# One-token decode on one Trainium2 core: K loaded after half of wq in runs of 16 KB, with a new pattern for its transposes, and wo's first 18 rows as one load

## The chip, the core and the metric

The kernel runs on one core of one Trainium2 chip. The metric is the device time of one execution in microseconds (us); several executions give a median. The profile beside it comes from one profiled execution. Of the engines, TensorE (PE) does the matrix products, VectorE (DVE) the transposes and most elementwise work, ScalarE (ACT) the exponentials and three small loads, GpSimd (POOL) fills constants at the start, and SyncE (SP) issues nearly all loads. All loads are moved by the core's 16 DMA engines.

## The reference

One token passes an attention block and an MLP block side by side. Cut to what matters:

```
xn  = layernorm(x)                                   # x: 1 x 1024
q   = xn @ wq                                        # wq: 1024 x 4096, 32 heads of 128
k,v = last 4096 positions of the caches, 4 kv heads, each shared by 8 heads
p   = softmax(q k^T / sqrt(128));  A = (p v) @ wo    # wo: 4096 x 1024
y   = layernorm(xn);  h = gelu(y @ w1 + b1)          # w1: 1024 x 3584
out = x + A + (h @ w2 + b2)                          # w2: 3584 x 1024
```

Everything is bf16. Each weight and each used cache element is used once, so some 39.9 MB have to come from memory: wq 8 MiB, w1 7, K 4, V 4, w2 7, wo 8.

## The kernel before

**Buffers.** `WA` holds wq, then w2, then wo's last rows. `W1` holds w1, then wo's other rows. `KV` holds K, then V. `KT` holds the transposed K. A load into a used buffer must wait until its readers are done, and that makes the order of the whole kernel.

**Loads.** Nearly all are issued by SP, in program order, and SP stops at each wait. First, without a wait: four K loads (L212, one for each kv head, 1 MiB, each of the 128 partitions getting one run of 8 KB), two halves of wq (L152, 4 MiB each, runs of 32 KB), two halves of w1 (L152, 3.5 MiB each). Then SP waits for the last K transpose (`C["kt"]`) and issues four V loads (L266). It waits for q to be done (`done["q"]`) and issues w2 in two loads. It waits for the first MLP product (`done["h"]`) and issues wo: 10 rows, 8 rows, then eight small loads of one split row (L275, `LOW`), then 6, 4, 2 and 1 rows. ("A row" of wo is here 128 partitions by 1024 columns.) Each load has its own semaphore, and PE waits for it where it first needs the data. Meanwhile ACT issues three small loads of its own at the start: the row x (2 KB), the row b2 (2 KB) and b1 (7 KB) (L161, L165). x and b2 go to the two rows of one tile, `XBRP`, and share the semaphore `s_x`; PE's first matmul waits for both.

**VectorE.** Its program order is: both layer norms and the spreading of xn into `XZ` and `YZ` (L223 to L253), a small constant (L256), then the four K transposes (L261), one for each K load:

```
for i in range(HKV):
    dve.wait_ge(s_k[i], 16)
    C["kt"] = DVE.mark(dve.transpose(KT[:, i * 4096:(i + 1) * 4096], KV[:, i * 4096:(i + 1) * 4096]))
```

A transpose here turns 32 x 32 blocks. After them come the copy of q out of PSUM (L282), its transpose (L284), eight copies into `QBD` (L291), the maximum of the scores, the transpose of the probabilities, and the MLP's GELU.

**TensorE.** Its program order is: x broadcast to all partitions (L373), two opening matmuls (L383), 64 matmuls over wq (L379 with `XZ`; 32 for each half), 28 over w1's first half (L379 with `YZ`), the 32 score matmuls over `KT` (L412, after `d_QBD`), 28 over w1's second half, the probabilities times V (L454), w2 (L464), then wo row by row as its loads land (L424 for 24 rows and for `LOW`, L430 for the last seven). Between the 24th and the 25th row ScalarE moves a part of the sum (L357). VectorE and ScalarE copy the result out (L363), SP stores it (L365).

Of the kernel before, what the change touches and what calls it, by code (L numbers as in the profile page):

```python
# [9 lines left out]
D = 1024  # L10
F = 3584
HQ = 32
HKV = 4
DH = 128
REP = HQ // HKV
SK = 65536
W = 4096
FC = F // 128
KC = D // 128
NQ = HQ * DH  # L20
W1_CHUNKS = [4, 4]
WQ_CHUNKS = [4, 4]
W2_CHUNKS = [16, 12]
WO_CHUNKS = [10, 8, 6, 4, 2, 1]
WO_HEAD = 4
WO_LOW = 18
XW = 136
QG = 520
# [22 lines left out]
def bass_parallel_sum__sliding_block_cached__mixer_channel_mlp__decode_kernel(  # L51
# [17 lines left out]
    pe, dve, act, pool, sp = nc.tensor, nc.vector, nc.scalar, nc.gpsimd, nc.sync  # L69

    def sems(name, n):
        return [nc.alloc_semaphore(f"{name}{i}") for i in range(n)]
# [2 lines left out]
    s_low = nc.alloc_semaphore("s_low")  # L75
    s_w1 = sems("s_w1", len(W1_CHUNKS))
    s_wq = sems("s_wq", len(WQ_CHUNKS))
    s_k = sems("s_k", HKV)
    s_wo = sems("s_wo", len(WO_CHUNKS))
    s_w2 = sems("s_w2", len(W2_CHUNKS))  # L80

    DVE = Track(nc, "S_DVE")
# [5 lines left out]
    def sb(name, shape, d):  # L88
        return nc.alloc_sbuf_tensor(name, shape, d)
# [40 lines left out]
    KV = sb("KV", [128, 16384], bf16)  # L130
    KT = sb("KT", [128, 16384], bf16)
    W1 = sb("W1", [128, KC * F], bf16)
    LOW = KT[0:64, 0:2 * D]
    WA = sb("WA", [128, KC * NQ], bf16)
# [8 lines left out]
    wq_p = A_wq.rearrange("(p r) n -> p r n", r=KC)  # L143
    w2_p = B_w2.rearrange("(p c) n -> p c n", c=FC)
    wo_p = A_wo.rearrange("(p j) n -> p j n", j=32)
    out_rows = out.rearrange("b s (a n) -> (b s a) n", a=2)

    C = {}

    def load_chunks(dst, src, chunks, width, semaphores, c0=0):  # L150
        for j, n in enumerate(chunks):
            sp.dma_start(  # L152
                dst[:, c0 * width:(c0 + n) * width].rearrange("p (c n) -> p c n", c=n),
                src[:, c0:c0 + n, :],
            ).then_inc(semaphores[j], 16)
            c0 += n
# [51 lines left out]
    POOL.mark(pool.memset(PT[:, 1024:1024 + 96], 0.0))  # L208
    C["consts"] = POOL.cnt

    for g in range(HKV):
        sp.dma_start(  # L212
            KV[:, g * 4096:(g + 1) * 4096],
            A_k_cache[0, g, SK - W:SK, :].rearrange("(p i) d -> p (i d)", p=128)).then_inc(s_k[g], 16)
    load_chunks(WA, wq_p, WQ_CHUNKS, NQ, s_wq)
    load_chunks(W1, w1_p, W1_CHUNKS, F, s_w1)

    def dve_wait():
# [37 lines left out]
    DVE.mark(dve.tensor_reduce(  # L256
        out=B32[:, :], in_=identf[:, :].rearrange("p (q r) -> p r q", q=4), axis=AX.X, op=ALU.add))

    for i in range(HKV):
        dve.wait_ge(s_k[i], 16)  # L260
        C["kt"] = DVE.mark(dve.transpose(KT[:, i * 4096:(i + 1) * 4096], KV[:, i * 4096:(i + 1) * 4096]))  # L261

    V = KV[:, :]
    sp.wait_ge(DVE.sem, C["kt"])
# [4 lines left out]
    sp.wait_ge(done["q"], 1)  # L269
    load_chunks(W2, w2_p, W2_CHUNKS, D, s_w2)  # L270
    sp.wait_ge(done["h"], 1)
    load_chunks(W1, wo_p, WO_CHUNKS[:2], D, s_wo)
    low_source = A_wo.rearrange("(u p j) n -> p u j n", u=2, j=32)[:, :, WO_MAIN, :]
    for first in (0, 1, 2, 3, 32, 33, 34, 35):
        sp.dma_start(  # L275
            LOW[first:first + 29:4, :].rearrange("p (u n) -> p u n", u=2),
            low_source[first:first + 29:4]).then_inc(s_low, 16)
    load_chunks(W1, wo_p, WO_CHUNKS[2:WO_HEAD], D, s_wo[2:], WO_LOW)
    load_chunks(WA, wo_p, WO_CHUNKS[WO_HEAD:], D, s_wo[WO_HEAD:], FC)

    dve.wait_ge(done["q"], 1)
# [127 lines left out]
    for b in range(2):  # L409
        for n in range(16):  # L410
            g, j = n // 4, n % 4
# [66 lines left out]
    c0 = 0  # L478
    for j, n in enumerate(WO_CHUNKS):
        if c0 == WO_LOW:  # L480
# [43 lines left out]
```

## Time and profile before

| | |
|---|---|
| median of 3 runs (lowest to highest) | 100.55 us (100.5 to 102.49) |
| the profiled execution: its own time, its span | 100.35 us, 99.1 us |
| busy: PE, DVE, ACT, POOL | 70.5, 37.5, 5.7, 6.5 us |
| DMA | 39.89 MB, mean 402 GB/s over the span |
| mean granted TensorE clock | 0.992 of full speed |

The span runs from the first to the last instruction; the time also holds 1.25 us around it. Busy times are sums over the span and say nothing of what waits for what; the DMA slices, the chain of waits and the start and landing times of single loads do. "Landing" is the time from the issue of a load until its semaphore is complete.

### The profile page before, as it was taken

Reading aid. Unit: us, or ns where it says so; the run is one execution under the profiler, and the core shown is the slowest. Engines: PE = TensorE matmul, PEld = TensorE weight load, DVE = VectorE, ACT = ScalarE, POOL = GpSimd, SP = SyncE. Lnnn points to the kernel's source line nnn. Section 1 sums busy time; section 2 is a strip of 40 time slices with the busy share of each in tenths; the row PEclk is TensorE's granted clock in tenths of the full one; section 3 lists DMA queues with packets and bytes.
Section 4 is the critical chain, followed back from the end, with each engine's and each line's share of the span. In section 5 each row is a group of like instructions: output and inputs, shape, how many; then the busy total and the mean of one; then the engine's idle time right before and its main releaser. Section 6 shows DMA issues by size and latency. Waiting matters only on the chain.

```text
span 99.1 us, 1197 instructions
## 1 busy us (share of the span) xinstructions
PE 70.5 (71%) x341; PEld 28.4 (29%) x341; DVE 37.5 (38%) x56; ACT 5.7 (6%) x11; POOL 6.5 (7%) x26
## 2 busy tenths in 40 slices
PE   0021000305999999999999999799999999979532
PEld 0000000002334433334444344233335445422210
DVE  0007998999999900091002543440024010000001
ACT  0500004200000000000000040000000000000021
POOL 6990000000000000000000000000000000000000
PEclk9999999999999999999999999999999999999996
DMA  2999999999999889889799999998999999999960
GB/s 26 397 426 418 430 436 436 489 476 463 450 423 397 370 382 544 370 382 544 301 423 420 423 522 423 423 423 370 476 476 422 388 397 427 423 402 440 397 256 4
DMA packets 3286, 39.89 MB, mean 402 GB/s; under 512 B 594, under 2 KB 596, under 8 KB 980
## 3 DMA queue, kind: packets, MB, share of 16 engines
q1 hardware_dynamic: 3076, 39.85, 95.0%
q10 hardware_dynamic: 208, 0.01, 0.1%
q8 instruction: 1, 0.02, 0.1%
q14 instruction: 1, 0.01, 0.0%
HBM read 39.86 MB, written 0.00 MB: 402 GB/s over the span
## 4 chain that ended last, share of the span: by engine, by line
DMA 46%; PE 40%; SPq 10%; issue 2%; DVE 0%
PE PS L379 31%; DMA WA<-in_A_wo_dram 26%; DMA WA<-in_A_wq_dram 20%; PE PS L412 7%; SPq L275 6%; SPq L152 2%; SPq L212 2%; PE PS L383 1%; PE PS L436 1%; DVE Pb L363 0%; PE PS L430 0%
## 5 line engine op out<-in xcount | busy, mean ns | idle before, releaser
L379 PE MATMUL PS<-WA,XZ 128*128 x64 | 17.9, 433 | 5.6 <-DMA WA<-in_A_wq_dram 5.2
L261 DVE STREAM_TRANSPOSE KT<-KV 128x4096 bf16<-128x4096 bf16 x4 | 17.4, 4409 | 0.0
L379 PE MATMUL PS<-W,YZ 128*128 x56 | 13.0, 381 | 0.0
L464 PE MATMUL PS<-WA,GT 128*64 x56 | 12.5, 380 | 0.0
L379 PEld LDWEIGHTS PS<-WA,XZ 128*128 x64 | 6.9, 108 | 17.0 <-issue 13.2
L383 PE MATMUL PS<-XBRP,HOT 1*128 1x512 bf16 x6 | 2.5, 454 | 9.5 <-DVE XZ L253 9.5
L454 PE MATMUL PS<-KV,PT 128*128 x32 | 8.5, 378 | 0.7 <-issue 0.7
L464 PEld LDWEIGHTS PS<-WA,GT 128*64 x56 | 6.0, 110 | 5.8 <-issue 1.2
L379 PEld LDWEIGHTS PS<-W,YZ 128*128 x56 | 5.2, 96 | 7.5 <-issue 2.5
L412 PE MATMUL PS<-KT,QBD 128*128 128x512 bf16 x32 | 7.1, 379 | 0.0
L424 PE MATMUL PS<-W,OT 128*32 128x512 bf16 x48 | 5.7, 380 | 1.8 <-DMA W<-in_A_wo_dram 1.8
L363 DVE CAST Pb<-PS 64x256 bf16<-64x256 f32 x1 | 0.4, 417 | 16.1 <-PE PS L430 16.1
L373 PE MATMUL PS<-XBRP,onesb 1*128 1x512 bf16 x2 | 1.0, 605 | 6.7 <-DMA XBRP<-in_B_b_dram 6.7
L297 DVE TENSOR_REDUCE MX<-PS 128x1 f32<-128x512 f32 x2 | 1.4, 692 | 10.0 <-PE PS L412 10.0
L454 PEld LDWEIGHTS PS<-KV,PT 128*128 x32 | 3.1, 96 | 6.1 <-issue 2.7
L223 DVE BATCH_NORM_STATS2 BN<-PS 128x6 f32<-128x512 f32 x2 | 1.3, 688 | 7.7 <-PE PS L373 7.7
L412 PEld LDWEIGHTS PS<-KT,QBD 128*128 128x128 bf16 x32 | 3.1, 98 | 3.7 <-issue 0.2
L383 PEld LDWEIGHTS PS<-XBRP,HOT 1*128 1x128 bf16 x6 | 0.5, 94 | 11.5 <-issue 11.5
L342 DVE SCALAR_TENSOR_TENSOR QBD<-PS,REC,GMASK 32x512 f32<-32x512 f32 x1 | 0.7, 739 | 7.9 <-PE PS L383 7.9
L424 PEld LDWEIGHTS PS<-W,OT 128*32 128x32 bf16 x48 | 2.1, 97 | 5.3 <-DMA W<-in_A_wo_dram 2.8
L282 DVE CAST Pb<-PS 128x512 bf16<-128x512 f32 x1 | 0.7, 692 | 7.4 <-PE PS L383 7.4
L308 ACT ACTIVATE Pb<-PS,NMB 128x1024 bf16<-128x1024 f32 x1 | 1.1, 1114 | 40.1 <-DVE NMB L305 40.1
(79 smaller groups left out, 33.4 us busy)
## 6 DMA issues: line engine op xcount, KB each, us to landing
WA<-in_A_wq_dram SPq DMA_DIRECT2D x2, 4096.0 KB, 24.4
W<-in_B_w_dram SPq DMA_DIRECT2D x2, 3584.0 KB, 41.0
KV<-in_A_k_cache_dram SPq DMA_DIRECT2D x4, 1024.0 KB, 7.9
KV<-in_A_v_cache_dram SPq DMA_DIRECT2D x4, 1024.0 KB, 20.6
WA<-in_B_w_dram SPq DMA_DIRECT2D x1, 4096.0 KB, 27.2
WA<-in_B_w_dram SPq DMA_DIRECT2D x1, 3072.0 KB, 34.2
W<-in_A_wo_dram SPq DMA_DIRECT2D x1, 2560.0 KB, 21.4
W<-in_A_wo_dram SPq DMA_DIRECT2D x1, 2048.0 KB, 25.9
```

The lines of the kernel that those rows point to most:

```text
L152: sp.dma_start(dst[:, c0 * width:(c0 + n) * width].rearrange("p (c n) -> p c n", c=n), src[:, c0:c0 + n, :],).then_inc(semaphores[j], 16)
L212: sp.dma_start(KV[:, g * 4096:(g + 1) * 4096], A_k_cache[0, g, SK - W:SK, :].rearrange("(p i) d -> p (i d)", p=128)).then_inc(s_k[g], 16)
L223: DVE.mark(dve.bn_stats(out=BN[:, 12 * n + 6 * i:12 * n + 6 * i + 6], in_=src[:, 512 * i:512 * i + 512]))
L261: C["kt"] = DVE.mark(dve.transpose(KT[:, i * 4096:(i + 1) * 4096], KV[:, i * 4096:(i + 1) * 4096]))
L275: sp.dma_start(LOW[first:first + 29:4, :].rearrange("p (u n) -> p u n", u=2), low_source[first:first + 29:4]).then_inc(s_low, 16)
L297: DVE.mark(dve.tensor_reduce(out=MX2[:, b:b + 1], in_=S[:, 512 * b:512 * b + 512], axis=AX.X, op=ALU.max))
L379: pe.matmul(bank(n), lhsT=vec[:, bass.ds(t + width * k, 128)], rhs=rhs_at(k, t), start=False, stop=False, skip_group_check=True)
L383: return pe.matmul(bank(n), lhsT=HOT[:, 8:136], rhs=XB[0:1, 0:8, :], start=start, stop=not start, skip_group_check=True)
L412: last = pe.matmul(bank(3 + b), lhsT=QBD[:, g * 512 + j * 128:g * 512 + j * 128 + 128], rhs=K5[:, g, 16 * b:16 * b + 16, j, :], start=(n = ...
L424: ins = pe.matmul(acc(a), lhsT=window(vec, c, a), rhs=rhs[:, a * 512:(a + 1) * 512], start=False, stop=stop, tile_position=(0, 32 * a), sk ...
L454: pe.matmul(bank(1), lhsT=PT[:, bass.ds(i * 256 + u * 32, 128)], rhs=V4[:, :, bass.ds(i * 8 + u, 1), :], start=False, stop=False, skip_gro ...
L464: pe.matmul(bank(7, 64), lhsT=GT[:, bass.ds(i * (4 * STEP) + (LEAD + STEP * (c0 + u) - ROW - a), 64)], rhs=W2[:, bass.ds(i * 4 * D + ((c0 ...
```

## The change

- **Order of loads.** SP issues wq's first half first, then K, then wq's second half and w1.
- **K in two loads.** Each load brings two kv heads, 2 MiB, with one run of 16 KB for each partition: partition 2m+g gets 64 consecutive positions of head g of the pair. There are two K semaphores in place of four.
- **The transposes.** There are still four of 128 x 4096 bf16, two behind each load, and they read contiguous columns. Because the partitions hold other positions, the output goes through a rearranged view of `KT`, so that `KT` ends up with the old layout. Within a block of 32 outputs the index is (m, a): a picks one of two regions of `KT` that lie 4096 elements (8 KB) apart, m steps by 2 elements (4 bytes) within the region. So no two consecutive outputs are neighbours in memory. The other transpose behind the same load fills the elements between.
- **wo.** The loads of 10 and of 8 rows become one of 18 rows (4.5 MiB, runs of 36 KB). PE waits for all 18 before the first of them.

```
-WO_CHUNKS = [10, 8, 6, 4, 2, 1]
-WO_HEAD = 4
+WO_CHUNKS = [18, 6, 4, 2, 1]
+WO_HEAD = 3
...
-    for g in range(HKV):
+    load_chunks(WA, wq_p, WQ_CHUNKS[:1], NQ, s_wq)
+    for c in range(2):
         sp.dma_start(
-            KV[:, g * 4096:(g + 1) * 4096],
-            A_k_cache[0, g, SK - W:SK, :].rearrange("(p i) d -> p (i d)", p=128)).then_inc(s_k[g], 16)
-    load_chunks(WA, wq_p, WQ_CHUNKS, NQ, s_wq)
+            KV[:, c * 8192:(c + 1) * 8192],
+            A_k_cache[0, 2 * c:2 * c + 2, SK - W:SK, :].rearrange("g (m i) d -> m g (i d)", m=64)).then_inc(s_k[c], 16)
+    load_chunks(WA, wq_p, WQ_CHUNKS[1:], NQ, s_wq[1:], WQ_CHUNKS[0])
     load_chunks(W1, w1_p, W1_CHUNKS, F, s_w1)
...
-    for i in range(HKV):
-        dve.wait_ge(s_k[i], 16)
-        C["kt"] = DVE.mark(dve.transpose(KT[:, i * 4096:(i + 1) * 4096], KV[:, i * 4096:(i + 1) * 4096]))
+    KTE = KT[:, :].rearrange("p (c a b m e) -> p c e b m a", c=2, a=2, b=128, m=16)
+    for c in range(2):
+        dve.wait_ge(s_k[c], 16)
+        for e in range(2):
+            first = c * 8192 + e * 4096
+            C["kt"] = DVE.mark(dve.transpose(
+                KTE[:, c, e], KV[:, first:first + 4096].rearrange("p (b m a) -> p b m a", b=128, m=16)))
...
-    load_chunks(W1, wo_p, WO_CHUNKS[:2], D, s_wo)
+    load_chunks(W1, wo_p, WO_CHUNKS[:1], D, s_wo)
...
-    load_chunks(W1, wo_p, WO_CHUNKS[2:WO_HEAD], D, s_wo[2:], WO_LOW)
+    load_chunks(W1, wo_p, WO_CHUNKS[1:WO_HEAD], D, s_wo[1:], WO_LOW)
     load_chunks(WA, wo_p, WO_CHUNKS[WO_HEAD:], D, s_wo[WO_HEAD:], FC)
```

## The prediction

> **What bounds the kernel now.** I read the page's slices first, then the waits of SP's queue, then the timeline around the change, and last the groups.
>
> ```profile
> DMA  2999999999999889889799999998999999999960
> ...
> SPq L266 <- DVE KT L261: 29.5, 1, 29.5
> ...
> 6.70 1.01 PE L373 MATMUL PS<-XBRP,onesb 1*128 1x512 bf16 x2 [6.70 <-DMA XBRP<-in_B_b_dram]
> 16.82 0.23 DVE L253 CAST XZ<-XNT 128x32 bf16<-128x32 f32 x1
> 17.18 17.41 DVE L261 STREAM_TRANSPOSE KT<-KV 128x4096 bf16<-128x4096 bf16 x4
> 23.39 18.30 PE L379 MATMUL PS<-WA,XZ 128*128 x64 [5.19 <-DMA WA<-in_A_wq_dram]
> 34.62 1.76 SPq L266 DMA_DIRECT2D KV<-in_A_v_cache_dram  x4
> ```
>
> The DMA engines are full from the second slice to the end: 39.9 MB in about 95 us, and the end follows wo's last load by 0.4 us. So the time is set by bytes, unless the stream of loads runs dry. That it doesn't is owed to a slack: V is issued at 34.62, the moment the last transpose ends, while the second w1 load (issued at 4.6, landing 45.0 later) still keeps the engines busy to about 49.1 (49.6, less 0.5 from last byte to semaphore). V's bytes follow without a gap. A load on idle engines starts about 1.0 us after its issue (K: issued at 0.80, first bytes at 1.8). So **V may be issued up to about 48**, 13.4 us later than now; every further us is one of idle DMA and goes into the time.
>
> PE is nearly as full: from 23.39 to 86.1 it has no gap over 0.8 us, and wo's first rows had landed at 84.1. It has hardly any slack of its own.
>
> **Part 1: larger runs.** Consecutive landings give the rates: V (8 KB runs) 3 MiB in 7.45 us, 2.48 us per MiB; w1 (28 KB runs) 3.5 MiB in 8.5, 2.43; wq (32 KB runs) 4 MiB in 9.75, 2.44. K's 4 MiB can gain 0.05 x 4 = 0.2 us; wo's first 18 rows (20 and 16 KB runs now) 0.1. The new K loads have a two-part source that no row shows. Nearest are the stretch with wo's uneven small loads, 383 GB/s, and the full stretches, 430: between 0.2 gained and 4 x 2.44 x (430/383 - 1) = 1.2 lost. I take 0.2, as each partition still gets one long run. **All the change can win here is 0.3 us.**
>
> **Part 2: wq's half ahead of K delays x.** ACT's three small loads are not edited, but they use the same 16 engines.
>
> ```profile
> XBRP<-in_A_x_dram ACTq DMA_DIRECT2D x1, 2.0 KB, 5.0
> XBRP<-in_B_b_dram ACTq DMA_DIRECT2D x1, 2.0 KB, 5.2
> B1T<-in_B_b_dram ACTq DMA_DIRECT2D x1, 7.0 KB, 7.4
> ...
> q10 hardware_dynamic: 32, 0.00, 5.5%
> ```
>
> x is issued at 0.80 and lands at 5.8; the store at the end, also 2 KB, takes 0.9. The last line is ACT's queue in the DMA view of the window 4.9 to 5.3: all 32 packets of x (16 of data, 16 of semaphore) lie there, and from 0.8 to 4.9 the view has none. The first K load lands at 5.6 (0.8 + 4.8). So x ran right behind the whole first K load, 1 MiB. The Trainium skill says as much ("DMA: Bandwidth & Descriptors", Queues, rings and completion order): an engine drains a whole packet of some 9 to 17 descriptors from one ring before it turns to the next; by it x would again wait for the whole first load.
>
> Now that load is 4 MiB of wq: x comes 9.75 - 2.48 = 7.3 us later. b2 trails x by 0.8 now, with 8 KB runs of K in between; with 16 KB runs I add 0.9. PE's L373 starts at 6.7 + 8.2 = 14.9. Bounds: nothing, if x gets in early, and 8.2; for a wait of only three 32 KB runs (1.2 us each, 9.75 us over 8 in an engine) 3.6. I take 8.2, for x's place right behind the first load. Everything on VectorE up to the transposes hangs on x without a gap: `XZ` at 25.2, **transposes from 25.4** instead of 17.18 (K has landed by 23). PE's wq loop starts at about 26.4, 3.0 later than 23.39; wq's second half, at 32.6 as now, is there in time. The first w1 product then ends at 51.5 (48.65 + 3.0, less 0.2 as PE has just run).
>
> **Part 3: scattered outputs.** Four transposes before and after, with no new DMA. The contiguous ones take 712 ns for 512 elements, 1245 for 1024, 4402 for 4096: 1.03 ns per element, so a gain is excluded.
>
> ```profile
> L246 DVE TENSOR_REDUCE XNT<-PT 128x8 f32<-128x1024 bf16 x1 | 1.9, 1944 | 0.0
> L312 DVE STREAM_TRANSPOSE PT<-Pb 128x1024 bf16<-128x1024 bf16 x1 | 1.2, 1245 | 1.3 <-ACT Pb L308 1.3
> L348 DVE TENSOR_REDUCE ON<-QBD 32x128 bf16<-32x512 f32 x1 | 1.0, 1028 | 0.0
> L297 DVE TENSOR_REDUCE MX<-PS 128x1 f32<-128x512 f32 x2 | 1.4, 692 | 10.0 <-PE PS L412 10.0
> L253 DVE CAST XZ<-XNT 128x32 bf16<-128x32 f32 x1 | 0.2, 227 | 0.0
> L351 DVE CAST OT<-PS 128x32 bf16<-128x32 f32 x1 | 0.2, 192 | 5.5 <-PE PS L473 5.5
> L336 DVE TENSOR_TENSOR GT<-HT,U 128x28 bf16<-128x28 f32 x1 | 0.2, 195 | 0.0
> L328 DVE TENSOR_TENSOR U<-U,HT 128x28 f32<-128x28 f32 x1 | 0.2, 188 | 0.0
> ```
>
> No transpose here writes scattered, so I bound it. Reads that hop at every element: L348 (512-byte hops) against L297 (contiguous), 512 elements each, (1028 - 692)/512 = 0.66 ns more; L246 (16-byte steps) against L312, 1024 each, 0.68. Writes that hop: L253 (64 bytes and more) against L351, 35 ns over 32, 1.1 ns; L336 (4-byte steps) against L328, 7 ns over 28, 0.25. Low 0.25, high 1.1. I take 0.68: the new pattern hops 8 KB at each element, as the long reads hop, though within a region it steps only 4 bytes. That is 16384 x 0.68 = **11.1 us more, transposes until 25.4 + 17.4 + 11.1 = 53.9** (low 46.9, high 60.8).
>
> The skill's "Vector Engine (DVE) Microarchitecture Reference" (Measured stream behaviour on trn2) speaks against this change: a port keeps its rate only for runs of two adjacent 4-byte words, and an output hopping 4 KiB every element costs 1.71 ns instead of 1.054. By it the extra is 10.7 us, an estimate; by its 2.50 for small steps it would be 23.7.
>
> **What the two parts do together.** Neither alone passes 48 (28.5 us from 17.2 is 45.7; 17.4 from 25.4 is 42.8). Together V is issued at 53.9, its bytes start at 55.0, and w1's end at 48.9: 6.1 us dry. The restart costs some 0.7 more (333 GB/s in the first 3.1 us against 430). **The stream shifts by 6.8**; wo's last load lands at 97.0 + 6.8 - 0.1 = 103.7. w2 is issued right behind V (q is done at 44.5), and wo at 72.9, while w2's bytes run to 82.8: neither adds a hole.
>
> Behind the transposes on VectorE stand the copy of q and `QBD` (42.04 to 44.95, 2.9 us), and PE's scores wait for these: 56.9. PE idles from 51.5. After the 5.2 us of idleness before 23.39 its first 40 matmuls took 11.72 us, against 6.65 for a later 28: 2.2 us too many. I charge that again. Scores end at 56.9 + 7.0 + 2.2 = 66.1, 10.5 later than 55.6, and w2 ends at 86.1 + 10.5 = 96.7.
>
> **Part 4: wo's 18 rows.** They land at 89.0 + 6.7 = 95.7, so the lost early start is hidden by PE being late. From 96.7: 36 matmuls, 4.0 (20 took 2.33, each further 0.105); `LOW` 0.5; six rows 1.3 (landed by 99.4); ScalarE's move 0.9; four rows 0.5; then the last two loads, 103.7, and 0.3: PE ends at about 104.3 against 97.4. Without that cover (no shift of DMA, PE at wo by 88.9) 18 rows from 89.0 end in time for the last loads within 0.2.
>
> **Sum:** 100.35 + 6.9 = 107.25 for an execution like the profiled one, whose time is 0.2 below the median of the runs: **107.5 us**. The likeliest case's own range is 104.5 to 110.5.
>
> **Rivals.**
>
> *Cheap scattered writes* (the other side). If the engine gathers the two alternating streams, the extra is 0.25 ns or less, the transposes end by 46.9, V is issued before 48, and the DMA never runs dry. For it: L336's 4-byte steps. Against: L253. It decides from 0.31 ns downwards (25.4 + 17.4 + 5.2 = 48). PE's wq loop is 3.0 late, w2 ends at 88.9, and wo's 18 rows land at 88.9 anyway: 100.3 us. A sentence of the same skill section is its support: a read alternating between two regions 16 KiB apart ran at the full rate; no run here shows it.
>
> *x is not held up by the whole load.* With 3.6 instead of 8.2, transposes run from 20.8 to 49.3, V's bytes start 1.4 late, and with 0.7 of restart the time is 102.5. Against: x's packets start just where the first K load ends.
>
> *Dear writes.* At 1.1 ns the transposes end at 60.8, all else 6.9 later than forecast: 114.4. For it: L253, the longest write here that hops at every element, though only 32 long.
>
> *The change does what its sizes suggest*, and fewer, longer runs pay by over 2 us: against it, full engines at 430 GB/s with any run length.
>
> **Chances.** Forecast 0.42, cheap writes 0.23, x early 0.12, dear writes 0.20, larger runs 0.03. A measurement of this kernel tells about 2% from no change: 98.5 to 102.6. Slower by over 2%: 0.42 + 0.20 + half of x early, 0.68; within 2%: 0.23 and the other half, 0.29; faster: 0.03. The range must reach just past the cheap writes and past the price at L253's row: 99.8 to 115.0.
>
> **What would show it.** L373 at about 15; transposes of 7.2 us each from 25.4; V issued near 54 and a hole in the DMA slices of some 6 us just before; scores from 57; SP's longest wait at L266 about 49 us. Transposes still of 4.4 us, or L373 still at 7, would each prove a step wrong and take most of the loss away.

## The result, and the profile after

The changed kernel takes **147.68 us** (median; 147.23 to 148.32) against 100.53 for the kernel before beside it: a ratio of 1.470 [1.465, 1.476], 47 us slower. The forecast was slower, 107.5, with a range to 115.0, so the direction was right, and so was the place (VectorE's transposes and the dry DMA behind them), and the size was far off. The profiled execution has a span of 146.3 us (99.1 before).

The page's slices, the wait that SP's queue had for V, and the costliest group of the changed kernel:

```profile
PEclk9999999999999975555555555556999999999999
DMA  5999999999998200000000000189999999798980
```

```profile
SPq L271 <- DVE KT L265: 89.6, 1, 89.6
```

```profile
L265 DVE STREAM_TRANSPOSE KT<-KV 128x4096 bf16<-128x4096 bf16 x4 | 72.7, 18464 | 0.0
```

One transpose takes 18.46 us instead of 4.40. SP stands at V's loads for 89.6 us instead of 29.5, the DMA slices show some 40 us without a byte, and PE's scores wait 48.05 us for `QBD`, which is behind the transposes on VectorE (the timeline's last column: idle time before, and what ended it):

```profile
10.66 1.00 PE L378 MATMUL PS<-XBRP,onesb 1*128 1x512 bf16 x2 [10.66 <-DMA XBRP<-in_B_b_dram]
21.13 72.75 DVE L265 STREAM_TRANSPOSE KT<-KV 128x4096 bf16<-128x4096 bf16 x4
93.91 1.97 SPq L271 DMA_DIRECT2D KV<-in_A_v_cache_dram  x4
96.63 9.24 PE L417 MATMUL PS<-KT,QBD 128*128 128x512 bf16 x32 [48.05 <-DVE QBD L296]
136.67 4.06 PE L429 MATMUL PS<-W,OT 128*32 128x512 bf16 x36
144.02 0.52 PE L435 MATMUL PS<-WA,OT 128*32 128x256 bf16 x12
```

x's product starts at 10.66 (6.70 before, 14.9 forecast), the transposes run from 21.13 to 93.88 (forecast 25.4 to 53.9), V is issued the moment they end, and most of what is behind keeps its old pace. **The loss is made by the longer transposes on VectorE and the 4 us of lateness ahead of them:** they end 59.3 us later than before (93.88 against 34.59), 13.4 of that is the forecast's slack, and the 45.9 that are left are nearly the whole loss of 47.

### The profile page after: what moved, and what is told of

The parts are those of the page before. It is cut to its first block, busy times and chain, and to the rows that moved or that the text cites. A ratio compares the mean times of both kernels' runs of the same rounds, so it can differ in the third digit from the quotient of the medians.

```text
span 146.3 us, 1194 instructions
## 1 busy us (share of the span) xinstructions
PE 71.7 (49%) x341; PEld 28.7 (20%) x341; DVE 92.6 (63%) x56; ACT 5.7 (4%) x11; POOL 6.5 (4%) x26
## 4 chain that ended last, share of the span: by engine, by line
DVE 58%; PE 32%; DMA 6%; issue 1%; ACT 1%; ACTq 0%
DVE KT L265 50%; PE PS L469 8%; PE PS L417 6%; DMA XBRP<-in_B_b_dram 6%; PE PS L459 6%; PE PS L384 4%; PE PS L429 4%; DVE BN L224 2%; DVE XNT L247 1%; DVE Pb L239 1%; DVE QBD L296 1%; DVE PT L243 1%; PE PS L378 1%; PE PS L435 1%; PE PS L388 1%
## 5 line engine op out<-in xcount | busy, mean ns | idle before, releaser
L265 DVE STREAM_TRANSPOSE KT<-KV 128x4096 bf16<-128x4096 bf16 x4 | 72.7, 18464 | 0.0
L417 PE MATMUL PS<-KT,QBD 128*128 128x512 bf16 x32 | 9.2, 461 | 48.0 <-DVE QBD L296 48.0
L384 PE MATMUL PS<-WA,XZ 128*128 x64 | 17.3, 416 | 2.3 <-DMA WA<-in_A_wq_dram 1.8
L417 PEld LDWEIGHTS PS<-KT,QBD 128*128 128x128 bf16 x32 | 3.6, 115 | 53.7 <-DVE QBD L296 48.5
```

The source lines that it names most:

```text
L265: C["kt"] = DVE.mark(dve.transpose(KTE[:, c, e], KV[:, first:first + 4096].rearrange("p (b m a) -> p b m a", b=128, m=16)))
L384: pe.matmul(bank(n), lhsT=vec[:, bass.ds(t + width * k, 128)], rhs=rhs_at(k, t), start=False, stop=False, skip_group_check=True)
L417: last = pe.matmul(bank(3 + b), lhsT=QBD[:, g * 512 + j * 128:g * 512 + j * 128 + 128], rhs=K5[:, g, 16 * b:16 * b + 16, j, :], start=(n = ...
```

## Experiments

The first theory is the forecast with one term corrected: the transposes' output pattern costs 3.43 ns per element ((18464 - 4409) / 4096), not 0.68, and nothing else is wrong but x's place in the queue. Its rival is that something else in the new arrangement slows the transposes (the new loads, the order, the layout of K). Each edit is against the kernel before unless it says otherwise.

### `plain`: the whole change, but with contiguous transposes

```
-            C["kt"] = DVE.mark(dve.transpose(KTE[:, c, e], KV[...].rearrange(...)))   # in the changed kernel
+            C["kt"] = DVE.mark(dve.transpose(KT[:, first:first + 4096], KV[:, first:first + 4096]))
```

> The whole change, but the four transposes write contiguous columns as before (KT then holds K in another order, so the scores are those of other positions; the work is the same). Theory S (only the scattered output costs): x lands some 4 us late as in the changed kernel, transposes take 4.4 us each from 21.1 to 38.7, V is issued at 38.7 and finds the DMA engines still full until 49; 100.0 to 100.8 us. Rival L (the order and the run length of the loads cost too): over 102.5 us, with a hole in the DMA slices or K landing after 24 us.

Measured: 101.39 us, ratio 1.003 [0.997, 1.009], where 100.0 to 100.8 was expected. With the output contiguous, the same loads in the same order give transposes of the old length. From its timeline and, last, its view of windows (length, busy time of PE, PEld, DVE, ACT, POOL, granted TensorE clock, DMA share, GB/s):

```profile
21.11 17.42 DVE L264 STREAM_TRANSPOSE KT<-KV 128x4096 bf16<-128x4096 bf16 x4
38.55 1.75 SPq L269 DMA_DIRECT2D KV<-in_A_v_cache_dram  x4
88.89 5.75 PE L427 MATMUL PS<-W,OT 128*32 128x512 bf16 x36 [2.78 <-DMA W<-in_A_wo_dram]
```

```profile
88.80:92.20 3.40, 3.31 (x16) 1.45 (x18) 0.00 (x0) 0.00 (x0) 0.00 (x0) 0.52 1.00 419
```

V is issued at 38.55, inside the slack to 48, although x is as late as in the changed kernel: that delay alone costs nothing. The last two lines show something else. PE waits 2.78 us for wo's 18 rows, and then the mean granted clock is 0.52 over 3.4 us: 36 matmuls take 5.75 us where the changed kernel took 4.06. `wo_alone`, below, takes that up.

### `scatter_alone`: only the output pattern

```
+    KTE = KT[:, :].rearrange("p (c a b m e) -> p c e b m a", c=2, a=2, b=128, m=16)
-        C["kt"] = DVE.mark(dve.transpose(KT[:, i * 4096:(i + 1) * 4096], KV[:, i * 4096:(i + 1) * 4096]))
+        C["kt"] = DVE.mark(dve.transpose(
+            KTE[:, i // 2, i % 2], KV[:, i * 4096:(i + 1) * 4096].rearrange("p (b m a) -> p b m a", b=128, m=16)))
```

> The kernel before (four K loads first, wo's 18 rows in two loads) with the scattered output pattern alone (the elements of K then stand for other positions; the work is the same). Theory S (the pattern makes the whole loss): transposes of 18.5 us each from 17.2 to about 90.3, 3.6 earlier than in the changed kernel, so 143 to 144.5 us. Rival (the long transposes need K's new loads or order): below 120.

Measured: 143.61 us, ratio 1.431 [1.425, 1.436]. Its timeline:

```profile
17.17 72.74 DVE L262 STREAM_TRANSPOSE KT<-KV 128x4096 bf16<-128x4096 bf16 x4
```

The old loads with the new output pattern give the same 72.7 us, and no new load, layout or order is needed for it: that rival falls. The 4.1 us that remain to the changed kernel are the 4.0 by which its transposes start later (21.13 against 17.17): once the slack is gone, x's delay counts in full.

### `one`: a dose of the pattern

```
+    dve.wait_ge(s_k[0], 16); dve.wait_ge(s_k[1], 16)          # in the changed kernel
+    # four contiguous transposes of 128x4096, and then one more, scattered:
+    C["kt"] = DVE.mark(dve.transpose(KTE[:, 0, 0], KV[:, 0:4096].rearrange("p (b m a) -> p b m a", b=128, m=16)))
```

> The whole change with one scattered transpose instead of four (the other three write contiguous columns; KT's order differs, the work is the same). Transposes should end at 21.1 + 3 x 4.4 + 18.5 = 52.8, about 1 us before the 53.9 that the prediction reckoned with. If the rest of the prediction's sum is right (V dry by 5 us, restart, cold PE, wo behind PE), the time is 106 to 107 us. Rival: the sum beyond the transposes is wrong, and the time is below 104 (the hole is filled otherwise) or above 109 (PE loses more).

Measured: 112.4 us, ratio 1.116 [1.114, 1.118]. The expectation counted three contiguous transposes and one scattered; the kernel as it ran holds four and one, and all begin only when both K loads have landed, at 22.9. So its numbers can't be held against the expectation as they stand, but against the forecast's sum, which wants only the time at which the transposes end. From the timeline and the slices:

```profile
40.33 18.34 DVE L268 STREAM_TRANSPOSE KT<-KV 128x4096 bf16<-128x4096 bf16 x1
58.69 1.95 SPq L274 DMA_DIRECT2D KV<-in_A_v_cache_dram  x4
```

```profile
DMA  6889999998999898930005999999799999979950
```

They end at 58.7 where the forecast had 53.9, so by its sum the time would be 107.25 + 4.8 = 112.05; 112.4 came, with the hole in the DMA slices just ahead of V. **Taken together, the terms behind the transposes (dry DMA, restart, scores, cold PE, wo) are right to 0.4 us;** single terms are not tested by it.

### `pat_a`, `pat_b`, `pat_c`: what in the pattern costs

Each of the three runs adds eight instructions of VectorE of half the size, with other output patterns, ahead of the kernel's own transposes. Two of the 24 lines:

```
+    DVE.mark(dve.transpose(KT[:, 0:4096].rearrange("p (n s) -> p s n", s=2)[:, 0, :], KV[:, 0:2048]))     # 4-byte step
+    DVE.mark(dve.transpose(KT[:, 0:8192].rearrange("p (a n u) -> p n a u", a=2, u=2)[:, 0:512], KV[:, 0:2048].rearrange("p (n a u) -> p n a u", a=2, u=2)))   # aligned pairs, two regions in turn
```

> The kernel before, with eight more transposes of 128 x 2048 bf16 ahead of the four K transposes, each on its own line with its own output pattern; the kernel's own time says nothing. By the contiguous rows one of 2048 takes 2.3 us; by the changed kernel the scattered pattern takes 9.2. Lines in order: contiguous; every second element (4-byte step); two regions 8 KB apart in turn, neighbours within a region; the changed kernel's pattern; the same elements with 16 of one region, then 16 of the other; two neighbours (4 bytes) of one region, then of the other; four neighbours (8 bytes) in turn; every eighth element (16-byte step). Theory H (hopping between regions costs): third and fourth 9.2, sixth half of the extra, seventh a quarter, second, fifth and eighth 2.3 to 3. Theory P (an output element whose neighbour is not written next costs): second, third, fourth, fifth and eighth all 9.2, sixth and seventh 2.3 to 5. Theory R (a short innermost row costs): third, fourth and sixth 9, fifth 3.2, second and eighth 2.3.

From VectorE's timeline, five of the eight: the 4-byte step, the changed kernel's pattern, 16 elements of one region before 16 of the other, aligned pairs in turn, the 16-byte step.

```profile
19.59 2.45 DVE L265 STREAM_TRANSPOSE KT<-KV 128x2048 bf16<-128x2048 bf16 x1
...
31.33 9.27 DVE L269 STREAM_TRANSPOSE KT<-KV 128x2048 bf16<-128x2048 bf16 x1
40.63 2.48 DVE L271 STREAM_TRANSPOSE KT<-KV 128x2048 bf16<-128x2048 bf16 x1
43.15 2.31 DVE L273 STREAM_TRANSPOSE KT<-KV 128x2048 bf16<-128x2048 bf16 x1
...
47.84 9.25 DVE L277 STREAM_TRANSPOSE KT<-KV 128x2048 bf16<-128x2048 bf16 x1
```

None of the theories fits all eight. Hops between regions are not the cost by themselves: pairs that hop at every pair are free (2.31, contiguous 2.30), and a 16-byte step with no hop to another region costs as much as the kernel's pattern (9.25 and 9.27). Half-written 4-byte words are not enough either: the 4-byte step leaves every word half-written and costs 2.45.

> As the other kernel of patterns, 2048 bf16 each, lines in order: a copy, contiguous; a copy with the changed kernel's output pattern; a transpose with two regions 8 KB + 64 bytes apart, 4-byte steps; with four regions 8 KB apart, 4-byte steps; every fourth element (8-byte step), one region; a transpose that reads the scattered pattern and writes contiguously; a transpose of 1024 float32, contiguous; of 1024 float32 with two regions 8 KB apart in turn. Theory W (any scattered write of VectorE costs 4.3 cycles an element): the copy's scattered line 9.2 us, the scattered read at most 3.6. Theory T (only the transpose is slowed): the scattered copy 2.2 to 3.6, transposes 9.2, and the scattered read 9.2 too if the pattern on either side spoils the turning. If two regions at equal low addresses conflict, the 64 bytes more bring the third line to 2.3 to 4; if not, 9.2. Float32: 1.2 contiguous; 4.6 if the price is per element, 1.9 if only two-byte writes are dear.

`pat_b`: contiguous copy, copy in the changed kernel's pattern, transpose with an 8-byte step, transpose that reads scattered and writes contiguous, and two transposes of 1024 whole 4-byte words (f32), contiguous and in two regions in turn.

```profile
17.64 0.69 DVE L261 COPY KT<-KV 128x2048 bf16<-128x2048 bf16 x1
18.36 5.33 DVE L263 COPY KT<-KV 128x2048 bf16<-128x2048 bf16 x1
...
42.35 4.76 DVE L269 STREAM_TRANSPOSE KT<-KV 128x2048 bf16<-128x2048 bf16 x1
47.15 2.34 DVE L271 STREAM_TRANSPOSE KT<-KV 128x2048 bf16<-128x2048 bf16 x1
49.52 1.25 DVE L273 STREAM_TRANSPOSE KT<-KV 128x1024 f32<-128x1024 f32 x1
50.80 1.95 DVE L275 STREAM_TRANSPOSE KT<-KV 128x1024 f32<-128x1024 f32 x1
```

It is the write, not the read (2.34 against 2.30), and the steps of 4, 8 and 16 bytes cost 2.45, 4.76 and 9.25, about twice as much each time. Whole 4-byte words hop between the regions for far less (1.95 us). That makes a rule, put down before `pat_c` ran: the times are as if the output were written in lines of 16 bytes, and each visit to a line that leaves a 4-byte word half-written cost (9247 - 180) / 2048 = 4.43 ns, beside 0.18 us fixed (the contiguous rows, 712 ns for 512 elements and 1245 for 1024, leave 0.18 for none); a 4-byte step makes one visit for four elements, an 8-byte step one for two, a 16-byte step or a hop to the other region one for each.

> The kernel before with eight more instructions of 2048 bf16 (or 1024 float32) ahead of the K transposes, one line each; the kernel's own time says nothing. In order: transposes that write pairs of neighbours, one pair in each 16 bytes, first on a 4-byte boundary, then off it (one element in each of two words); float32 with 16-byte steps; with 8-byte steps; copies of bf16 with 4-byte steps; with 16-byte steps; with aligned pairs in two regions in turn; a copy of float32 to bf16 with two regions in turn. Theory P (what costs is a 16-byte line that is left with a half-written 4-byte word, 4.4 ns for each visit): aligned pairs 2.3 us, pairs off the boundary 4.7, float32 below 2.0 in both. Theory N (only the number of neighbouring elements per visit counts): both kinds of pairs alike. For the copies, by theory P 16-byte steps cost at least twice 4-byte steps, and aligned pairs no more than 2.3.

`pat_c`: transposes that write one aligned pair into every 16 bytes, one pair off the word boundary into every 16 bytes, and 1024 whole 4-byte words (f32) with a 16-byte and with an 8-byte step; last, a cast of 1024 f32 to bf16 in two regions in turn.

```profile
17.99 2.30 DVE L261 STREAM_TRANSPOSE KT<-KV 128x2048 bf16<-128x2048 bf16 x1
20.33 4.71 DVE L263 STREAM_TRANSPOSE KT<-KV 128x2048 bf16<-128x2048 bf16 x1
25.08 2.00 DVE L265 STREAM_TRANSPOSE KT<-KV 128x1024 f32<-128x1024 f32 x1
27.11 1.25 DVE L267 STREAM_TRANSPOSE KT<-KV 128x1024 f32<-128x1024 f32 x1
...
35.70 2.74 DVE L275 CAST KT<-KV 128x1024 bf16<-128x1024 f32 x1
```

| pattern of 2048 bf16 (transposes) | half-word visits | 0.18 + visits x 4.43 ns, but no less than 2.30 | measured, us |
|---|---|---|---|
| contiguous; aligned pairs or 8-byte runs in turn; one aligned pair per 16 bytes | 0 | 2.30 | 2.30, 2.31, 2.31, 2.30 |
| 4-byte step; 16 of one region, then 16 of the other | 512 | 2.45 | 2.45, 2.48 |
| 8-byte step; pair off the word boundary | 1024 | 4.72 | 4.76, 4.71 |
| the changed kernel's; neighbours in two regions; four regions; regions 64 bytes further apart; 16-byte step | 2048 | 9.25 | 9.27, 9.23, 9.24, 9.31, 9.25 |

The two cases that tell, the pair on and the pair off the word boundary, came out as the rule says; lines of 8 or of 32 bytes would not fit the steps of 4, 8 and 16. What the machine does in those 4.43 ns no run shows. Copies pay about half as much per element: 5.33 us in the changed kernel's pattern, 4.76 with the 16-byte step (in `pat_c`, where the 4-byte step took 1.32). Why is left open.

### `wo_alone`: only wo's 18 rows in one load

```
-WO_CHUNKS = [10, 8, 6, 4, 2, 1]
-WO_HEAD = 4
+WO_CHUNKS = [18, 6, 4, 2, 1]
+WO_HEAD = 3
```

> The kernel before with wo's first 18 rows as one load, nothing else. PE is at wo at 86.1 and would wait for the 18 rows until 88.9; 36 matmuls, the split row, six rows, ScalarE's move and the last rows then run without a wait. By the prediction's step 0 to 0.2 us slower than before; by the profile with contiguous outputs (its chain ends on this stretch) about 1 us slower: 101.5.

Measured: 101.55 us, ratio 1.009 [1.007, 1.012]: slower by 1.0 us, where the forecast had 0.2 without cover. Timeline and windows:

```profile
89.12 5.75 PE L424 MATMUL PS<-W,OT 128*32 128x512 bf16 x36 [2.44 <-DMA W<-in_A_wo_dram]
```

```profile
89.10:93.40 4.30, 4.28 (x25) 1.96 (x27) 0.00 (x0) 0.00 (x0) 0.00 (x0) 0.60 0.98 411
```

Waiting for 18 rows costs no bytes, but it leaves PE idle for 2.4 us, and over the 4.3 us that follow the mean granted clock is 0.60: 36 matmuls take 5.75 us instead of 4.06. PE comes out of wo's rows too late for the last loads. Shorter waits did not lower the clock: after the 1.83 us that PE of the changed kernel waits for wq's second half, and after 1.25 us before wo's six rows in the kernel before, it stayed at 1.00. Nor is it lost each time behind the 18 rows: the one execution of 100.41 us has a mean granted clock of 0.996, the other eleven, 101.2 and above, lie at 0.979 to 0.990, save one of 1.0 at 101.69, which stays unexplained; so the clock is the likely cause of this loss, and not shown to be all of it. (In `plain` the one of 100.08 us has 1.0, the three above 101 have 0.980 to 0.983.)

### `order_alone` and `runs_alone`: the loads

`order_alone` puts wq's first half ahead of the four old K loads; `runs_alone` leaves K first, in the two new loads.

```
+    load_chunks(WA, wq_p, WQ_CHUNKS[:1], NQ, s_wq)                  # order_alone
     for g in range(HKV):
         ...
-    load_chunks(WA, wq_p, WQ_CHUNKS, NQ, s_wq)
+    load_chunks(WA, wq_p, WQ_CHUNKS[1:], NQ, s_wq[1:], WQ_CHUNKS[0])

+    for c in range(2):                                              # runs_alone; contiguous transposes
+        sp.dma_start(KV[:, c * 8192:(c + 1) * 8192],
+            A_k_cache[0, 2 * c:2 * c + 2, SK - W:SK, :].rearrange("g (m i) d -> m g (i d)", m=64)).then_inc(s_k[c], 16)
```

> The kernel before with wq's first half ahead of K's four old loads, nothing else; it computes the same. x should land near 10.5 as in the changed kernel and the transposes run from 21.1 to 38.6, inside the slack that ends at 48: 100.2 to 100.8, no difference. Rival: PE, which now starts wq at 22 and must wait for its second half near 32.5, loses its fast rate there and the chain ends over 1 us later.

Measured: 100.65 us, ratio 1.000 [0.996, 1.004]. Its transposes start at 21.17 and V is issued at 38.61: the same 4 us as in the changed kernel, and they cost nothing while the transposes are short.

> The kernel before with K in the two loads of 16 KB runs at the old place, ahead of wq; contiguous transposes (KT's columns then stand for other positions, the work is the same); wo as before. By the rates of the prediction the longer runs win 0.2 us: 100.3. Rival: the larger first runs start up slower (in the kernel that reads KT scattered wq's first half landed 0.5 us later than before), and it is level or up to 0.5 slower.

Measured: 101.12 us, ratio 1.009 [1.006, 1.013], a small loss, where the forecast had a gain of 0.2. Windows of this kernel at its start (the kernel before moves 41 GB/s in the first and 390 in the second):

```profile
0.80:2.40 1.60, 0.00 (x0) 0.00 (x0) 0.00 (x0) 0.00 (x0) 1.37 (x5) 1.00 0.01 1
2.40:6.00 3.60, 0.00 (x0) 0.00 (x0) 0.00 (x0) 1.28 (x1) 3.40 (x10) 1.00 1.05 355
```

As the first load of the program the two-part load brings its first bytes later (one-part loads, of 8 KB runs in the kernel before and of 32 KB runs in the changed one, begin at 1.8 us): 41 - 1 over 1.6 us and 390 - 355 over 3.6 us are 0.19 MB less, some 0.45 us at 430 GB/s, and PE's end is 0.6 later (97.68 against 97.08). In the changed kernel that doesn't arise, since wq's half comes first.

### `readside_kfirst` and `readside_rows`: the new loads without any scattered write

Both take the new K loads first, transpose contiguously, and let PE read `KT` in the order that undoes the layout. `readside_kfirst` hops between the two heads' columns at every element; `readside_rows` reads rows of 16 elements with a 4-byte step, and the exponential's output puts the positions right.

```
-    K5 = KT[:, :].rearrange("p (g i j k) -> p g i j k", g=HKV, i=32, j=4)
+    K6 = KT[:, :].rearrange("p (c e i j m a) -> p c a j i m e", c=2, e=2, i=32, j=4, m=16)   # kfirst
+    K6 = KT[:, :].rearrange("p (c e i j m a) -> p c a j i e m", c=2, e=2, i=32, j=4, m=16)   # rows
```

> K first, in the two loads of 16 KB runs, then both halves of wq; contiguous transposes; the score matmuls read KT in the scattered order instead (16 positions by two regions 8 KB apart); wo in two loads as before. This computes the same scores as before. Theory 1 (TensorE reads scattered columns at full rate, as VectorE did): 100.2 to 100.8 us, no gain from the longer runs beyond 0.2. Theory 2 (it reads them slower): the 32 score matmuls take over 12 us and the time is over 104. On x: if x runs behind the whole first load (8 runs of 16 KB per engine), PE's first matmul starts at 9 to 9.5; if it is first served near 5 us and then after each single run, at 7.3 to 8.

> As the kernel in which the score matmuls read KT scattered, but in another order: 16 elements with 4-byte steps, then 16 of the next 4096 columns; the exponential writes its output in the order that undoes it, so the result is the reference's. Theory 1 (TensorE loses only where every element hops): 32 score matmuls in about 7 us, the time 100.2 to 101. Theory 2 (any step above one costs TensorE): over 10 us for the scores, and 101.5 to 108.

Measured: 108.12 us (ratio 1.075 [1.073, 1.078]) and 101.37 us (1.012 [1.007, 1.017]). The scores, one line of the timeline of each:

```profile
49.02 17.29 PE L414 MATMUL PS<-KT,QBD 128*128 128x512 bf16 x32
```

```profile
49.28 7.08 PE L415 MATMUL PS<-KT,QBD 128*128 128x512 bf16 x32
```

Hopping at every element costs PE 17.29 instead of 7.08 us; rows of 16 read at the full rate. The second kernel still lies above the 100.2 to 101 expected; what is left of its loss is about that of `runs_alone`, which has the same loads (1.009).

### `mended`: the change with the layout undone by PE's reads

The changed kernel's order and K loads, contiguous transposes, the reads and the exponential of `readside_rows`, and wo in its old two loads.

```
-            C["kt"] = DVE.mark(dve.transpose(KTE[:, c, e], KV[...].rearrange(...)))          # against the changed kernel
+            C["kt"] = DVE.mark(dve.transpose(KT[:, first:first + 4096], KV[:, first:first + 4096]))
-WO_CHUNKS = [18, 6, 4, 2, 1]
+WO_CHUNKS = [10, 8, 6, 4, 2, 1]
```

> The changed kernel with its two costs taken out: contiguous transposes, the score matmuls reading KT in rows of 16 with 4-byte steps and the exponential undoing the order; wo's first 18 rows in two loads again. wq's half stays ahead of K, K comes in runs of 16 KB, and the result is the reference's. What is left is the gain of the longer runs, 0.2 us by the prediction: 100.3, against 100.5 before. Rival: the late x or the wait inside wq costs after all, over 101.

Measured: 100.51 us, ratio 1.000 [0.995, 1.005]. The whole loss is gone and nothing is won. The page's DMA slices:

```profile
DMA  6599999999999899889799999999999999999960
```

The engines are full from the third slice to the end here and from the second in the kernel before, and larger K runs don't make the stream measurably faster. No version here beats the kernel before.

## Why the prediction was right or wrong

**The mechanism of the loss was right, and the term that decides it was mis-sized: the price of the scattered output.** (A second step, x behind the whole first load, was wrong too, and worth 4.3 us the other way; it is taken up below.) The forecast took 0.68 ns per element, from rows of scattered *reads*, with bounds of 0.25 and 1.1 from *writes* of 28 and 32 elements. Measured: 3.43 ns. The transposes take 72.7 us, not 28.5. The bounds failed because neither end came from an operation like this one: no row had a transpose with a scattered output, and the runs show that reads say nothing of it (2.34 us, free) and that another operation pays another price (a copy about half). L253, the "dear" row, was a cast; a cast that hops at every element took 2.74 us for 1024 in `pat_c`, about 2.5 ns each, the same order as L253's 1.03 + 1.1. So that row was roughly right for casts and no bound for transposes. L336's 4-byte step, the support of the cheap rival, is, by the rule above, cheap for a reason that does not carry over: four of its elements share a 16-byte line, and the hop between regions takes just that away.

The sentence on the Trainium skill ("Vector Engine (DVE) Microarchitecture Reference", Measured stream behaviour on trn2) failed with it. That table is of 4-byte words, and for far hops of these the trace agrees: 1024 f32 in two regions in turn took 1.95 us in `pat_b`, (1.95 - 0.18) / 1024 = 1.73 ns each, near the page's 1.71. For short steps of a transpose it does not: single f32 words with an 8-byte step were free (1.25 us, as contiguous), where the page asks for two adjacent words, and a 16-byte step took (2.00 - 0.18) / 1024 = 1.78 ns each, where the page's small step, a longer one, has 2.50. For half a word it has no row, and the forecast used it for one.

**Put into the same sum, the measured terms give the time.** Last matmul at 104.3 by the forecast; less 4.3 for x (transposes from 21.13, not 25.4), plus 44.2 for the transposes (72.7, not 28.5): 144.2. Measured: 144.02 + 0.52 = 144.5. In time 107.25 + 39.9 = 147.2, against 147.68.

**Part 1, the size of the gain.** Not contradicted: `mended` and `order_alone` show no gain that can be told from none, and the 0.3 of the forecast is too small to be told from none. The bound on the other side (a two-part source can lose) was met only where that load comes first: 0.6 us in `runs_alone`.

**Part 2, x behind the whole first load.** Wrong: x did not wait for the load's end. x's product starts 3.96 late, not 8.2; the bound at 3.6 us was near. The DMA view of the changed kernel, window 5.0 to 8.1, has ACT's queue as

```profile
q10 hardware_dynamic: 32, 0.00, 0.7%
```

with all 32 packets of x, and none before 5.0, while wq's first half has 9.75 us of bytes and needs until about 11.5. Its windows up to 5.9 us count 48 runs of wq, three of eight for each of the 16 engines, and none of x's packets. From there 16 runs of wq alternate with 16 packets of ACT's queue, 1.2 us a turn: x's data from 6.1, then x's semaphore, b2's data, b2's semaphore. So the queues take turns run by run, and it isn't the end of a load that lets x in. In the kernel before it only happened to come there, and the forecast took that for the rule. The bound had the three runs right and its 3.6 us by luck, for it took the whole wait as lateness, though x had waited before too: x's data come only 1.2 us later (4.9 before), and the rest comes of the 32 KB runs that now stand ahead of x's semaphore, of b2 and of b2's semaphore. Why it is three runs at first is not shown (`plain`, `order_alone` and `mended` have the same three).

With K's two-part load first it is otherwise. From the loads of `runs_alone` and its timeline:

```profile
XBRP<-in_A_x_dram ACTq DMA_DIRECT2D x1, 2.0 KB, 1.9
XBRP<-in_B_b_dram ACTq DMA_DIRECT2D x1, 2.0 KB, 6.3
7.84 1.01 PE L375 MATMUL PS<-XBRP,onesb 1*128 1x512 bf16 x2 [7.84 <-DMA XBRP<-in_B_b_dram]
```

x's packets all run before K's first bytes, x lands at 2.7, and PE waits for b2 alone; in `readside_kfirst` it is the same (1.8 and 6.1 after issue, L375 at 7.63). PE's first matmul reads only x's row, but the semaphore that it waits for counts b2 too. No run gives x a semaphore of its own; in the changed kernel x lands at 8.1 and b2 at 10.5.

The page on which the forecast leaned (the Trainium skill's "DMA: Bandwidth & Descriptors", Queues, rings and completion order) has an engine drain a whole packet of 9 to 17 descriptors before it turns; this trace has turns after one run of 32 KB, or three at the start. The error worked against the other one, by 4.3 us.

**The slack to about 48.** Right: V issued at 38.6 costs nothing (`order_alone`, ratio 1.000), V at 58.7 costs what the sum says (`one`), V at 93.9 likewise.

**Cold PE.** Charged at 2.2 us for the scores; measured 9.24 - 7.07 (before) = 2.2. From the windows of the changed kernel: the first eleven score matmuls, and those behind.

```profile
96.60:101.00 4.40, 4.37 (x11) 1.62 (x12) 0.00 (x0) 0.00 (x0) 0.00 (x0) 0.50 1.01 423
101.20:106.00 4.80, 4.80 (x23) 2.07 (x22) 0.78 (x2) 0.00 (x0) 0.00 (x0) 1.00 1.13 478
```

The granted clock is 0.50 for 4.4 us, and then 1.00.

**Part 4, wo.** Half right. In the changed kernel the 18 rows land at 135.4, 1.3 ahead of PE at 136.67, so they are hidden as forecast. "Without that cover 0.2" was wrong: `wo_alone` lost 1.0, since the sum counted when the rows come and not the lower clock seen behind 2.4 us of idleness, although the forecast charged just that for the scores.

**The chances.** The rival "x is not held up by the whole load" was true, and "dear writes" was true beyond its own price. Both were priced as alternatives to each other, and the second one's end, 1.1, was taken as an end of the range when only rows of another operation stood behind it.

## What to carry to other kernels

A bound from the nearest rows is a bound only where they are the same operation, with the same element size and direction; where no such row exists, the upper end is open, and a price that is paid 16,384 times is worth carrying as open in the range. Let a VectorE transpose write 2-byte results in aligned pairs, or at least let four neighbours in a row fall into one 16-byte line, and put a necessary permutation on a read: a transpose's, or a matmul's in rows of 16. And when a merged load lets TensorE idle even for 2.4 us, count some 3.4 us of matmuls behind it at half the clock; here 1.8 us did no harm, and one execution of twelve had no loss.

## What the runs showed of the hardware that was not expected

- A VectorE transpose that writes single 2-byte elements, each into another 16-byte line, takes 4.4 ns for each, 4.2 times the contiguous time; in aligned pairs the same hops are free.
- TensorE's mean granted clock was 0.52 over 3.4 us and 0.60 over 4.3 us after idle stretches of 2.8 and 2.4 us, and the next 36 matmuls took 5.75 us instead of 4.06.
- A matmul whose moving operand hops at every 2-byte element takes 17.29 / 32 = 0.54 us for 512 columns; in rows of 16 with a 4-byte step 0.22, the full rate.
- As a program's first load, one with two parts of 16 KB runs brought its first bytes after 2.4 us where one-part loads of 8 KB and of 32 KB runs had begun at 1.8.
